# An S4 mixer and MLP kernel: parts of the spectra in the free dimension, taps of two channels per matmul, one transposing transfer per block and chunk

## The chip, the cores and the metric

The kernel runs on one core of a Trainium2 chip. TensorE (PE) multiplies matrices into PSUM; VectorE (DVE), ScalarE (ACT) and GpSimd (POOL) compute on SBUF; SyncE (SP) issues nearly all transfers. The metric is the device time of one execution in microseconds. The median of three runs of the kernel before is 296.92 us (296.33 to 298.66).

## The reference

x has 2048 positions of 512 channels. Two residual blocks follow each other: a long convolution along the positions, whose taps K come from a state-space model with 128 complex states per channel, and an MLP of width 1376. Cut to what matters:

```python
logdA = dt * (A_re + 1j * A_im); dB = dt * Bc
P = jnp.exp(logdA[:, :, None] * l[None, None, :])     # l = 0..2047, rounded to bf16
K = jnp.einsum("dn,dnl,dn->dl", Cc, P, dB).real       # taps of each channel
y = irfft(rfft(pad(u)) * rfft(pad(K)))[:L] + u * Dskip
h = x + y        # u = layernorm(x)
h2 = h + (gelu(layernorm(layernorm(h)) @ w1 + b1) @ w2 + b2)
```

## The kernel before

**Planner.** Every operation is recorded by `add` with its engine, a cost and what it reads and writes. `Sched.run` then orders all of them by a model of the engines, with priorities from the table RANK and PSUM slots from a pool of four (1024 fp32 each), and the order it finds is emitted per engine. It also models PE's clock and a wait at every 256th PE instruction. Because of the helpers, all evictions from PSUM (`evac`) show as L536 on ScalarE or L538 on VectorE, whichever the planner chose, and all transfers as L548.

**Arena.** SBUF is one array `ar`; buffers are byte ranges in it, and many share bytes at different times. E and I hold, for each of NCH = 4 chunks of 128 channels, the real and imaginary parts of exponentials: 20 rows "A" (EA, IA) and 33 rows "B" (EB, IB).

**Taps.** The exponent of position l is split into one of 20 A rows and one of 33 B rows, so the taps of one channel are a 20 x 33 product over the 128 states. `aexps` makes the magnitudes of A in PSUM tiles that accumulate, each fourth row from the one before (LD, two tiles), with an Exp on ScalarE; `bexps` makes those of B. `chain` accumulates phases in PSUM, takes Sin on ScalarE and multiplies on VectorE (L1013, L1014). `kgen` (L1035, L1036) multiplies per channel: 20 weight columns, 33 moving columns, real and imaginary part accumulating, four channels in four column tiles of PE. It evicts into Kg (three buffers). `kspec` (L1080) applies the weights W (a cosine and sine transform along one digit of the position) to Kg over 20 rows in four row tiles, evicts into AK (two buffers) and writes to AK_d in DRAM. `kload` reads it back with the other digit on the partitions and does the second transform stage (L1096).

**Spectra of u.** `austage` does the first stage for the normalised input and writes AU_d in DRAM; `xspec0` (block 0, all channels, L917) and `xspec` (block 1, one chunk at a time, L935) read it back and do the second stage. The stage's weights T have 64 columns of a real and 64 of an imaginary part for each f, so that both parts of a spectrum lie on the partitions. A third copy of 64 columns lets `TT_` form a matmul with the parts swapped, and so each spectrum is kept twice, as X and as Xs. Block 1 uses two buffer pairs XB and two KF1 for the four chunks.

**Inverse.** `inverse` multiplies the tap spectrum with X and Xs on VectorE (L1114), transforms back with TP1 and TP2 over 128 rows (L1123) and evicts into Z. For six of the eight calls, Z is written to Z_d in DRAM and read back into ZT with (q, f) on the partitions. For chunks 2 and 3 of block 0 (TURN) the matmul has its operands exchanged, the result is evicted in four pieces, transposed by PE (L1138) and evicted again.

**Tail and MLP.** `tail` adds x and the last inverse stage in PSUM (L1208, L1213), takes statistics on VectorE (L1218), normalises (L1232, L1234) and transposes (L1239). `mlp` follows: L1257 with Gelu (L1259), then L1274 and the residual (L1276). Each 1024 positions (block) have two tails and two MLP passes. Block 0's taps act on block 0; block 1 needs the taps and spectra of both.

Of the kernel before, what the change touches and what calls it, by code (L numbers as in the profile page):

```python
# [9 lines left out]
ACT = mybir.ActivationFunctionType  # L10
# [13 lines left out]
NKG = 3  # L24
# [124 lines left out]
class VS(V):  # L149
# [15 lines left out]
    "0S": 4, "0A": 87, "0.01A": 322, "0.02S": 140, "0.03A": 55, "0.04S": 263, "0.05S": 334, "0.1S": 264, "0.1A": 228, "0P": 137, "0.05P": 299,  # L165
    "0.1D": 85, "0.7D": 202, "0.75P": 153, "0.6P": 340, "0.72P": 246, "0.3D": 22, "0.1P": 309, "0.2P": 335, "0.05A": 239, "0.06A": 339, "0.07A": 247,
    "0.08A": 330, "0.09A": 269, "0.5D": 304, "0.5P": 353, "0.2A": 341, "0.2D": 96, "1.01A": 359, "1.015A": 184, "1.02A": 238, "1.025A": 240,
    "1.03A": 59, "1.035A": 251, "1.04A": 208, "1.045A": 24, "1.05A": 116, "1.055A": 75, "1.06A": 150, "1.065A": 49, "1.07A": 106, "1.075A": 349,
    "1.08A": 162, "1.085A": 40, "1.09A": 35, "1.095A": 104, "1.1A": 237, "1.105A": 213, "1.11A": 79, "1.115A": 102, "1.12A": 338, "1.125A": 326,
    "1.13A": 220, "1.135A": 115, "1.14A": 180, "1.145A": 42, "1.15A": 205, "1.155A": 90, "1.16A": 278, "1.165A": 361, "0.4A": 84, "0.4P": 229,  # L170
    "0.401A": 163, "0.4D": 12, "0.41D": 21, "0.42D": 274, "0.6A": 291, "0.6D": 248, "0.5S": 13, "0.55D": 44, "0.55S": 261, "1.5D": 317, "1.3P": 307,
    "1.55D": 354, "1.4P": 206, "1.5P": 38, "1.2D": 3, "1.201D": 60, "1.202D": 195, "1.203D": 172, "8D": 270, "8S": 165, "0.95P": 64, "0.95A": 110,
    "1.05P": 320, "1.15P": 305, "1.25P": 54, "1.25A": 127, "1.35P": 157, "1.35A": 99, "1.45P": 232, "1.45A": 289, "1.55P": 315, "1.55A": 188,
    "1.65P": 257, "1.65A": 161, "1.75P": 187, "1.75A": 10, "1.85P": 105, "1.85A": 37, "8A": 7, "1.3A": 70, "1.3D": 345, "1.7P": 32, "1.71P": 266,
    "1.9A": 114, "2.05P": 221, "1.8P": 133, "1.81P": 192, "2.11P": 145, "2P": 199, "2A": 211, "2D": 178, "2.1P": 203, "2.1A": 262, "2.1D": 46,
    "2.2P": 357, "2.2A": 210, "2.2D": 28, "2.3P": 48, "2.3A": 19, "2.3D": 148, "2.5P": 119, "2.5A": 61, "2.5D": 181, "2.6P": 355, "2.6A": 168,
    "2.6D": 36, "2.7P": 66, "2.7A": 300, "2.7D": 83, "2.8P": 113, "2.8A": 128, "2.8D": 234, "2.9P": 301, "2.9A": 212, "2.9D": 135, "2.94A": 89,
    "3.2D": 225, "4.1D": 280, "2.98A": 132, "2.99D": 86, "2.96A": 325, "2.97A": 362, "2.95A": 303, "4.5P": 151, "1.72P": 292, "3.4D": 302,
    "3.401D": 124, "3.402D": 313, "3.403D": 209, "3.5P": 53, "3.5A": 231, "3.5S": 173, "3.501P": 43, "3.501A": 295, "3.501S": 6, "4P": 306, "4A": 268,
    "4D": 243, "4.1P": 58, "4.1A": 65, "4.2P": 324, "4.2A": 319, "4.2D": 57, "4.3P": 242, "4.3A": 103, "4.3D": 331, "4.5A": 108, "4.5D": 236,  # L180
    "4.6P": 332, "4.6A": 218, "4.6D": 15, "4.7P": 226, "4.7A": 297, "4.7D": 352, "4.8P": 71, "4.8A": 73, "4.8D": 179, "4.9P": 155, "4.9A": 189,
    "4.9D": 277, "4.1S": 327, "4.101P": 283, "4.101A": 154, "4.101S": 97, "4.2S": 69, "4.201P": 351, "4.201A": 216, "4.202P": 344, "4.202A": 107,
    "4.203P": 50, "4.203A": 201, "5.1P": 166, "5.1A": 316, "5.11P": 29, "5.11A": 1, "5.11D": 147, "5.2P": 146, "5.2A": 190, "5.2S": 88, "6.2P": 260,
    "6.2A": 214, "6.2S": 20, "5.25S": 275, "5.25P": 33, "5.25A": 77, "5.3D": 170, "5.3P": 204, "5.3A": 284, "5.3S": 139, "9.1P": 25, "9.1A": 39,
    "9.11P": 346, "9.11A": 323, "9.11D": 167, "9.2P": 253, "9.2A": 136, "9.2S": 272, "10.2P": 224, "10.2A": 196, "10.2S": 23, "9.25S": 318,
    "9.25P": 68, "9.25A": 347, "9.3D": 142, "9.3P": 254, "9.3A": 62, "9.3S": 185, "13.1P": 56, "13.1A": 30, "13.11P": 81, "13.11A": 348, "13.11D": 174,
    "13.2P": 31, "13.2A": 94, "13.2S": 249, "14.2P": 227, "14.2A": 342, "14.2S": 333, "13.25S": 294, "13.25P": 45, "13.25A": 296, "13.3D": 76,
    "13.3P": 329, "13.3A": 169, "17.1P": 98, "17.1A": 120, "17.11P": 130, "17.11A": 121, "17.11D": 186, "17.2P": 143, "17.2A": 175, "17.2S": 52,
    "18.2P": 197, "18.2A": 215, "18.2S": 271, "17.25S": 217, "17.25P": 158, "17.25A": 112, "17.3D": 152, "17.3P": 285, "17.3A": 308, "25S": 11,
    "25.02S": 336, "25.04S": 259, "25.06S": 360, "25.1S": 82, "25.12S": 51, "25.14S": 356, "25.16S": 41, "40S": 92, "40.1S": 267, "40.2S": 67,  # L190
    "40.3S": 255, "40.5S": 95, "40.51S": 17, "40.52S": 256, "40.53S": 200, "40.54S": 350, "40.55S": 118, "40.56S": 138, "40.57S": 123, "40.58S": 282,
    "40.59S": 250, "42A": 343, "42P": 80, "30P": 288, "30D": 74, "30A": 279, "31P": 252, "31D": 273, "31A": 233, "70P": 290, "70A": 293, "70D": 122,
    "70S": 314, "50S": 111, "50P": 276, "50A": 194, "51S": 337, "51P": 244, "51A": 328, "52D": 141, "52P": 281, "52A": 14, "52S": 193, "53S": 5,
    "53P": 93, "53A": 101, "54S": 126, "54P": 182, "54A": 27, "55D": 9, "55P": 191, "55A": 0, "55S": 156, "56S": 286, "56P": 223, "56A": 47,
    "57S": 310, "57P": 134, "57A": 16, "58D": 241, "58P": 125, "58A": 129, "58S": 72, "59S": 159, "59P": 171, "59A": 149, "60S": 235, "60P": 258,
    "60A": 312, "61D": 8, "61P": 222, "61A": 198, "61S": 311, "65S": 245, "65.02S": 34, "65.04S": 219, "65.06S": 164, "65.1S": 18, "65.12S": 117,
    "65.14S": 144, "65.16S": 26, "71P": 298, "71A": 91, "71D": 183, "71S": 265, "66P": 2, "66D": 78, "66A": 176, "67P": 358, "67D": 160, "67A": 177,
    "73P": 131, "73A": 207, "73D": 230, "73S": 109, "74P": 321, "74A": 287, "74D": 100, "74S": 63,
# [33 lines left out]
class Sched:  # L232
# [45 lines left out]
    def run(self, nslots):  # L278
# [47 lines left out]
        while av:  # L326
# [84 lines left out]
def kernel(ctx, tc, A_u, A_A_re, A_A_im, A_B_re, A_B_im, A_C_re, A_C_im, A_log_dt, A_Dskip,  # L411
# [509 lines left out]
    def TT_(f, r):  # L921
        return T.ap()[:, f, r:r + 2].rearrange("p a b -> p (a b)")

# [481 lines left out]
```

## Time and profile before

| | |
|---|---|
| median of 3 runs | 296.92 us |
| the profiled execution | 297.31 us, of it span 295.5 us |
| PE, busy | 232.2 us (79%), 3337 matmuls |
| VectorE, busy | 185.5 us (63%), 392 instructions |
| ScalarE, busy | 198.0 us (67%), 257 instructions |
| GpSimd, busy | 46.0 us (16%) |
| DMA | 34.15 MB in 57191 packets, 43873 of them under 512 B |
| evictions of 1024 fp32 values | ScalarE 61 at 1.03 us, VectorE 31 at 1.22 us |

Busy times of PE overlap its weight loads, and matmuls are pipelined, so a busy PE need not be at its peak. The chain of waits goes back from the last instruction to what released each step. "issue" in it is time in which an engine waited for nothing that the profile shows. In the table of stretches each row gives busy time and count for each engine, then the granted PE clock, the mean busy share of the 16 DMA engines and the GB/s.

### The profile page before, as it was taken

How to read it: one execution, taken by the hardware profiler on the slowest of the kernel's cores; microseconds unless marked ns; L12 is line 12 of the kernel's file. 1: busy time of each engine (PE TensorE's matmuls, PEld its weight loads, DVE VectorE, ACT ScalarE, POOL GpSimd, SP SyncE). 2: the span in 40 equal slices, each digit the busy share in tenths (PEclk: the TensorE clock that was granted, in tenths of full speed). 3: DMA queues.
4: the chain of work that ended last, by engine and by line, in shares of the span. 5: the costliest groups of instructions: out<-in, count | busy, mean ns of one | idle time of the engine just before them, and what ended most of it. 6: DMA issues, size and time to landing. Idle time of an engine off the chain costs nothing.

```text
span 295.5 us, 8030 instructions
## 1 busy us (share of the span) xinstructions
PE 232.2 (79%) x3337; PEld 140.1 (47%) x3360; DVE 185.5 (63%) x392; ACT 198.0 (67%) x257; POOL 46.0 (16%) x213
## 2 busy tenths in 40 slices
PE   6204948788997797499977629799999999898983
PEld 2101313344576546487855226578674334443431
DVE  3999999999986798035736784656850375311021
ACT  5988999999956994157984848685528338832700
POOL 9992102996000000000000000000000000000000
PEclk9999998999999999979999958999999999999999
DMA  7700113799101679997896300656564011002011
GB/s 145 265 0 2 35 41 91 195 231 341 35 4 57 192 167 241 239 235 257 249 219 155 71 1 0 176 141 201 144 159 110 0 46 29 1 18 57 0 35 36
DMA packets 57191, 34.15 MB, mean 116 GB/s; under 512 B 43873, under 2 KB 52034, under 8 KB 57154
## 3 DMA queue, kind: packets, MB, share of 16 engines
q1 hardware_dynamic: 55954, 33.24, 42.3%
q8 instruction: 26, 0.43, 0.6%
q10 hardware_dynamic: 1200, 0.39, 0.5%
q14 instruction: 11, 0.09, 0.1%
HBM read 19.47 MB, written 13.63 MB: 112 GB/s over the span
## 4 chain that ended last, share of the span: by engine, by line
PE 47%; DVE 22%; issue 10%; ACT 9%; DMA 5%; SPq 3%; POOL 2%; DVEq 0%; ACTq 0%; POOLq 0%
PE ps L1274 12%; PE ps L1257 9%; ACT ar L536 6%; PE ps L1123 5%; DVE ar L593 4%; PE ps L1036 3%; SPq L548 3%; PE ps L1035 3%; DVE ar L878 3%; DVE ar L598 3%; DVE ar L538 3%; PE ps L997 2%; PE ps L1080 2%; DMA ar<-AU_d 2%; DVE ar L1218 2%
## 5 line engine op out<-in xcount | busy, mean ns | idle before, releaser
L536 ACT CAST ar<-ps 128x1024 bf16<-128x1024 f32 (+3 forms) x91 | 75.2, 889 | 49.5 <-DVE ar L1218 9.8
L538 DVE CAST ar<-ps 128x1024 bf16<-128x1024 f32 (+2 forms) x33 | 38.8, 1194 | 19.0 <-PE ps L1096 12.8
L1257 PE MATMUL ps<-ar 128*128 128x512 bf16 (+1 forms) x170 | 40.6, 384 | 2.8 <-ACT ar L536 1.4
L1274 PE MATMUL ps<-ar 128*128 128x512 bf16 (+1 forms) x168 | 40.1, 379 | 3.1 <-DVE ar L1276 2.7
L1114 DVE TENSOR_TENSOR ar<-ar 128x1024 bf16<-128x1024 bf16 x48 | 30.1, 688 | 17.1 <-PE ps L1123 14.6
L1259 ACT ACTIVATE ar<-ps,ar 128x512 bf16<-128x512 f32 (+1 forms) x44 | 29.7, 689 | 14.5 <-PE ps L1257 14.1
L1003 ACT ACTIVATE ar<-ps 128x1024 bf16<-128x1024 int16 x36 | 35.5, 1042 | 3.5 <-PE ps L997 3.0
L584 POOL TENSOR_SCALAR ar<-ar 128x128 bf16<-128x128 bf16 (+5 forms) x40 | 30.5, 783 | 15.6 <-DMA ar<-ar 10.4
L1276 DVE TENSOR_TENSOR ar<-ps,ar 128x512 bf16<-128x512 f32 x16 | 11.0, 690 | 32.7 <-PE ps L1274 25.6
L1257 PEld LDWEIGHTS <-ar 128*128 128x128 bf16 (+1 forms) x176 | 17.6, 101 | 22.1 <-issue 4.3
L1274 PEld LDWEIGHTS <-ar 128*128 128x128 bf16 (+1 forms) x176 | 16.7, 97 | 22.8 <-issue 4.9
L1036 PE MATMUL ps<-ar 128*20 128x33 bf16 x512 | 20.0, 248 | 6.6 <-issue 6.6
L1218 DVE BATCH_NORM_STATS2 ar<-ps 128x6 f32<-128x512 f32 x16 | 11.1, 697 | 21.7 <-PE ps L1213 16.7
L1123 PE MATMUL ps<-ar 128*128 128x128 bf16 x384 | 24.1, 219 | 0.6 <-DVE ar L1114 0.3
L997 PE MATMUL ps<-ar 128*32 128x256 f16 x560 | 21.4, 275 | 3.8 <-ACT ar L1003 1.6
L1123 PEld LDWEIGHTS <-ar 128*128 128x128 bf16 x384 | 22.3, 98 | 3.3 <-DVE ar L1114 1.0
L1036 PEld LDWEIGHTS <-ar 128*20 128x20 bf16 x512 | 17.8, 125 | 8.2 <-issue 8.2
L997 PEld LDWEIGHTS <-ar 128*32 128x32 f16 x560 | 13.9, 97 | 12.6 <-issue 12.1
L1035 PE MATMUL ps<-ar 128*20 128x33 bf16 x512 | 19.7, 249 | 0.2
L1014 DVE TENSOR_TENSOR ar<-ar 128x1024 bf16<-128x1024 bf16 x26 | 17.8, 702 | 1.6 <-ACT ar L1003 1.5
L1013 DVE TENSOR_TENSOR ar<-ar 128x1024 bf16<-128x1024 bf16 x26 | 18.1, 709 | 0.9 <-ACT ar L1003 0.8
L1035 PEld LDWEIGHTS <-ar 128*20 128x20 bf16 x512 | 17.5, 124 | 0.5 <-issue 0.2
(92 smaller groups left out, 307.8 us busy)
## 6 DMA issues: line engine op xcount, KB each, us to landing
AU_d<-ar SPq DMA_DIRECT2D x16, 256.0 KB, 4.6
ar<-AU_d SPq DMA_DIRECT2D x8, 512.0 KB, 5.9
AK_d<-ar SPq DMA_DIRECT2D x16, 256.0 KB, 4.2
ar<-AK_d SPq DMA_DIRECT2D x8, 512.0 KB, 5.6
Z_d<-ar SPq DMA_DIRECT2D x12, 256.0 KB, 3.2
ar<-Z_d SPq DMA_DIRECT2D x6, 512.0 KB, 4.6
ar<-in_A_u_dram SPq DMA_DIRECT2D x4, 512.0 KB, 7.1
ar<-in_A_u_dram SPq DMA_DIRECT2D x16, 128.0 KB, 5.4
```

The lines of the kernel that those rows point to most:

```text
L536: act.copy(out_fn(), in_fn())
L538: dve.tensor_copy(out_fn(), in_fn())
L584: en.tensor_scalar(a, b, f(s1), f(s2), op0, op1)
L997: pe.matmul(pst(p)[32 * g:32 * g + 32, 256 * j:256 * j + 256], lhsT=W2[DELTAS.index(d)].ap(), rhs=S2[g].ap()[:, ch0:ch0 + 256], start=Fals ...
L1003: add("ACT", c_act(1024), lambda e, p=p, sc=sc, cs=cs: act.activation(sc[cs].ap().rearrange("p a b -> p (a b)"), pst(p, i16).rearrange("p ...
L1035: pe.matmul(o, lhsT=Ar.ap()[:, :, d], rhs=Br.ap()[:, :, d], start=True, stop=False, tile_position=(0, 32 * g))
L1036: pe.matmul(o, lhsT=Ai.ap()[:, :, d], rhs=Bi.ap()[:, :, d], start=False, stop=True, tile_position=(0, 32 * g))
L1114: add("DVE", c_dve(1024, 2), lambda e, kf=kf, x=x, pr_=pr_, f0=f0: dve.tensor_tensor(pr_.ap(), kf[f0:f0 + 8].ap(), x[f0:f0 + 8].ap(), ALU. ...
L1123: pe.matmul(pst(p)[:, 128 * k:128 * k + 128], lhsT=a, rhs=b_, start=(n == 0), stop=(n == len(jobs) - 1))
L1257: pe.matmul(pst(p)[:fs, 512 * z:512 * z + 512], lhsT=w1s[dc].ap()[:, fc * P:fc * P + fs], rhs=ybuf.ap()[:, dc, :], start=(dc == 0), stop=( ...
L1259: add("ACT", c_act(512, 1), lambda e, p=p, z=z, fc=fc, fs=fs: act.activation(hT.ap()[:fs, fc, :], pst(p)[:fs, 512 * z:512 * z + 512], ACT. ...
L1274: pe.matmul(pst(p)[:, 512 * z:512 * z + 512], lhsT=hT.ap()[:fs, fc, 128 * t:128 * t + 128], rhs=w2s[fc].ap()[:fs], start=(fc == 0), stop=( ...
```

## The change

The second stage now makes real and imaginary parts side by side in the free dimension (two matmuls of 64 weight columns, one in each half of PE's columns, for two values of f). The swapped spectrum is no copy any more but a reversed index in the product. The inverse contracts over 64 rows in two row tiles with three half-size tables TP, always with the channels on the output partitions, and one transfer per block and chunk transposes Z from SBUF to SBUF; Z_d, TURN's path and Xs are gone. `kgen` handles two channels per matmul: 52 weight columns (12 rows that are padding or an earlier buffer's end, then 20 rows of each channel) by 66 moving ones; the cross products are left unused, and W is zero on the first 12 rows. `aexps` uses three PSUM tiles (each sixth row from the one before), and EA and IA keep the two halves of a chunk's channels apart. Kg and AK have four buffers, XB and KF1 four each. RANK has new values, and two constants of the planner's model change.

```diff
-NKG = 3
+NKG = 4
 RANK = {
...
-                        blk.append(t + 2.8 + 0.6 * min(8.0, max(0.0, dma_busy - t)))
+                        blk.append(t + 3.3 + 0.4 * min(5.0, max(0.0, dma_busy - t)))
...
-    T = take(bf16, 16, 3, 64)
-    TP1 = take(bf16, 16, P)
-    TP2 = take(bf16, 16, P)
+    T = take(bf16, 16, 2, 64)
+    TP = [take(bf16, 8, P) for _ in range(3)]
...
-    XR = [(VS(X0, c), VS(X0s, c)) for c in range(NCH)]
-    Kg = [take(bf16, NB, 32) for _ in range(NKG)]
-    AK = [take(bf16, 16, CW) for _ in range(2)]
+    XR = [VS(X0, c) for c in range(NCH)]
+    Kg = [take(bf16, NB, 2, 32) for _ in range(2)] + [at(lo, bf16, NB, 2, 32) for lo in (X0s.lo, BA0 + 12288)]
+    AK = [take(bf16, 16, CW) for _ in range(2)] + [at(BA0 + 4096 * n, bf16, 16, CW) for n in (1, 2)]
...
-    EA = [at(E0 + c * ESZ, bf16, NA, CW) for c in range(NCH)]
+    EA = [at(E0 + c * ESZ, bf16, 2, NA, 64) for c in range(NCH)]
...
-        for f in range(16):
+        for f in range(8):
...
-                    pe.matmul(pst(p)[:, 512 * r:512 * r + 512], lhsT=TT_(f, r), rhs=X0.ap()[:, f, :], start=True, stop=True)
...
-            evac(lambda f=f: multi(X0.lo + 1024 * f, 16384, bf16, 2, 512), lambda p=p: pst(p).rearrange("p (c d) -> p c d", c=2), 1024, [p], [X0[f], X0s[f]])
+                    for h in range(2):
+                        fmat(pst(p)[64 * h:64 * h + 64, 512 * r:512 * r + 512], 2 * f + h, r, X0.ap()[:, 2 * f + h, :])
...
+            evac(lambda f=f: X0[2 * f:2 * f + 2].ap().rearrange("p a b -> p (a b)"), lambda p=p: pst(p), 1024, [p], [X0[2 * f:2 * f + 2]])
+    def fmat(o, f, r, rhs):
+        pe.matmul(o, lhsT=T.ap()[:, f, r, :], rhs=rhs, start=True, stop=True, tile_position=(0, 64 * (f & 1)))
+    def fstage(v):
+        for f0 in range(0, 16, 8):
...
+                for k in range(0, 8, 2):
+                    for r in range(2):
+                        for h in range(2):
+                            fmat(pst(p)[64 * h:64 * h + 64, 128 * (k + r):128 * (k + r) + 128], f0 + k + h, r, v.ap()[:, f0 + k + h, :])
...
+        fstage(X)
...
-    KIS = [[(0, 11), (11, 11)], [(22, 10)]]
+    KIS = [[(0, 7), (7, 7)], [(14, 7), (21, 7)], [(28, 4)]]
...
+                    for i in range(n):
+                        for z, (a, b) in enumerate(pair):
+                            for t in range(2):
+                                o = pst(p)[64 * t:64 * t + 32 + NA, 512 * nb:512 * nb + 2 * NB * n].rearrange("p (k i) -> p k i", i=n)[:, :, i]
+                                pe.matmul(o, lhsT=a[:, :, 32 * t + i0 + i], rhs=b[:, :, :, 32 * t + i0 + i], start=(z == 0), stop=(z == 1), tile_position=(0, 64 * t))
...
+        fstage(kf)
...
-            for kf, (X, Xs) in pairs:
-                for x, TPx in ((X, TP1), (Xs, TP2)):
+            for kf, X in pairs:
+                for sw in range(2):
...
+                        a, b_, o = (q.ap().rearrange("p (a r) d -> p a r d", r=2) for q in (kf[f0:f0 + 8], X[f0:f0 + 8], pr_))
+                        dve.tensor_tensor(o, a, b_[:, :, ::-1, :] if sw else b_, ALU.mult)
...
+                for k in range(4):
+                    for n, (q, w0, w1) in enumerate(jobs):
+                        for r, w in enumerate((w0, w1)):
+                            for h in range(2):
+                                rows = slice(64 * h, 64 * h + 64)
+                                b_, a = TP[w].ap()[rows, f0 // 2 + k, :], q.ap()[rows, 2 * k + r, :]
+                                pe.matmul(pst(p)[:, 512 * h + 128 * k:512 * h + 128 * k + 128], lhsT=a, rhs=b_, start=(n == 0 and r == 0), stop=(n == len(jobs) - 1 and r == 1), tile_position=(64 * h, 0))
...
-            evac(lambda z=z: z.ap().rearrange("p a b -> p (a b)"), lambda p=p: pst(p), 1024, [p], [z])
-            dma("SP", lambda z=z, f0=f0: Z_d[b][c][:, f0:f0 + 8, :], lambda z=z: z.ap(), 262144, [z], [("Z", b, c, fh)])
...
-        dma("SP", lambda: zt.ap(), lambda: zv, 524288, [("Z", b, c, 0), ("Z", b, c, 1)], [zt], k=1.2)
+            evac(lambda f0=f0: zw.ap()[:, :, f0:f0 + 8].rearrange("p q (k h) -> p q k h", h=2), lambda p=p: pst(p).rearrange("p (h k q) -> p q k h", h=2, k=4), 1024, [p], [zw])
+        add("SP", 0.55, lambda e: nc.sync.dma_start(zt.ap(), zw.ap().rearrange("p (s q) f -> p s (q f)", s=16), transpose=True), r=[zw], w=[zt], byts=524288)
...
-    XB = [(at(BA0 + 26624 + 8192 * n, bf16, 16, CW), at(BA0 + 26624 + 8192 * n + 4096, bf16, 16, CW)) for n in range(2)]
-    KF1 = [at(BA0 + 43008 + 4096 * n, bf16, 16, CW) for n in range(2)]
+    XB = [at(BA0 + 26624 + 4096 * n, bf16, 16, CW) for n in range(4)]
+    KF1 = [at(lo + 4096 * n, bf16, 16, CW) for lo in (BA0 + 43008, X0s.lo) for n in range(2)]
...
-    Jk = at(Kg[0].lo, f32, 16, 64)
+    Jk = at(Kg[0].lo, f32, 8, 64)
...
-    TS(T, T, 1.0, None, ALU.mult, n=1024, mode=4, oap=lambda: T.ap()[:, :, 2, :], iap=lambda: T.ap()[:, :, 0, :], pr=2.99)
-    AC(TP1, TPc[0], ACT.Sin, scale=pmS, oap=lambda: TP1.ap().rearrange("p a b -> p (a b)"), iap=lambda: low16(TPc[0]), tbl=True, pr=2.96)
-    AC(TP2, TPc[1], ACT.Sin, scale=SINSC, oap=lambda: TP2.ap().rearrange("p a b -> p (a b)"), iap=lambda: low16(TPc[1]), tbl=True, pr=2.97)
+    for n, (q, sc) in enumerate(((0, SINSC), (0, -SINSC), (1, SINSC))):
+        AC(TP[n], TPc[q], ACT.Sin, scale=sc, oap=lambda n=n: TP[n].ap().rearrange("p a b -> p (a b)"), iap=lambda q=q: low16(TPc[q]), tbl=True, pr=2.96 + 0.003 * n)
...
-        inverse(1, c, [(KF0[c], XB[c % 2]), (KF1[c % 2], (XR[c][0], XR[c][1]))], ZT1[c], 2 * c, 52 + 3 * c)
+        inverse(1, c, [(KF0[c], XB[c]), (KF1[c], XR[c])], ZT1[c], 52 + 3 * c)
```

## The prediction

> **What bounds the kernel now.** The profiled execution took 297.31 us (span 295.5, so 1.8 lie around it); the median of the runs is 296.92. I sum against 297.3 and carry the difference over. First I read busy time by stretch of 20 us (columns: length; busy us and instructions of PE, its weight loads, VectorE, ScalarE, GpSimd; granted clock; DMA share; GB/s).
>
> ```profile
> 60.00:80.00 20.00, 17.41 (x314) 9.23 (x314) 19.68 (x30) 19.55 (x22) 11.14 (x13) 1.00 0.70 214
> 80.00:100.00 20.00, 17.10 (x726) 14.65 (x718) 14.82 (x26) 13.83 (x17) 0.52 (x1) 1.00 0.22 62
> 100.00:120.00 20.00, 15.41 (x420) 10.26 (x417) 16.46 (x18) 14.50 (x16) 0.00 (x0) 1.00 0.86 205
> 120.00:140.00 20.00, 16.52 (x507) 14.13 (x496) 6.36 (x9) 9.49 (x12) 0.00 (x0) 0.91 0.92 240
> 140.00:160.00 20.00, 16.30 (x380) 14.10 (x377) 12.74 (x16) 17.31 (x22) 0.00 (x0) 1.00 0.84 221
> 160.00:180.00 20.00, 10.74 (x83) 5.80 (x74) 14.06 (x53) 12.07 (x18) 0.00 (x0) 0.75 0.19 44
> ...
> 200.00:220.00 20.00, 19.79 (x220) 14.32 (x222) 14.95 (x22) 8.93 (x11) 0.00 (x0) 1.00 0.57 158
> ```
>
> Four regimes: up to 80 us VectorE and ScalarE are full; from 80 to 160 no engine is, but DMA is at 0.84 to 0.92; from 160 to 180 (the first tails) PE is half idle at a low clock; from 180 on PE is full. Next, the chain of waits (start, length, what) and the waits of PE's weight loads, where a row is who waited for whom, us, times, longest.
>
> ```profile
> 108.43 5.27 DMA ar<-AK_d
> 113.75 1.07 PE ps L1096 x16
> ...
> 118.69 1.09 issue
> ...
> 122.11 2.77 issue
> ...
> 143.49 3.41 ACT ar L536 x4
> ...
> 157.86 1.11 PE ps L1138 x16
> ...
> 199.37 1.84 PE ps L1123 x32
> ...
> 231.19 0.56 PE ps L1213 x4
> ```
>
> ```profile
> PEld L1036 <- issue: 8.2, 8, 2.9
> ```
>
> The DMA view (queue: packets, MB, share; then issues with count, size, us to landing):
>
> ```profile
> q8 instruction: 26, 0.43, 0.6%
> ...
> AK_d<-ar SPq DMA_DIRECT2D x16, 256.0 KB, 4.2
> ar<-AK_d SPq DMA_DIRECT2D x8, 512.0 KB, 5.6
> Z_d<-ar SPq DMA_DIRECT2D x12, 256.0 KB, 3.2
> ar<-Z_d SPq DMA_DIRECT2D x6, 512.0 KB, 4.6
> ```
>
> The middle stretch is a sequence of latencies: `kgen` on PE with gaps in which PE has nothing to issue, trips through AK_d, evictions on ScalarE. The gaps fit instruction fetch: 26 packets carry 0.43 MB, 16.5 KB each, and PE's 3337 matmuls with 3360 loads in 26 portions are 258 instructions each. `kgen` has 1024 matmuls and 1024 loads, 8 such portions, and 8 gaps of 8.2 us together. The chain shows four of its matmuls every 0.07 us, so a portion lasts 128 x 17.5 ns = 2.24 us, less than its successor takes to come while DMA is loaded.
>
> **Part by part.** *Taps.* `kgen` goes from 1024 matmuls (20 weight columns, 33 moving, four column tiles) to 512 (52 and 66, two tiles). If issue alone sets the pace, 17.5 ns each, it falls from 17.9 to 9.0 us; if weight columns do, 17.5 x 52/20 = 45.5 ns and 23.3 us. I take the moving columns, 35 ns and 17.9 us as before: twice the columns at half the tiles, between the ends. A portion of 256 instructions then lasts 4.5 us, and there are 4: half of the gaps go, **-4.1**, all on the chain (bounds 0 and -8.2). Its evictions grow from 726 + 330 to 924 + 924 + 264 elements per chunk: at 773 ns per 726 some 1.1 us more per chunk, hidden by ScalarE, which is busy for 9.5 of 20 us there; without that cover it is +4.4.
>
> *Spectra.* `xspec0` drops from 16 evictions of 1024 to 8, `xspec` of block 1 from 16 to 8; the swapped copy Xs is now read by a reversed access pattern. The chain products already read reversed blocks (L1013, 709 ns) and cost what the plain ones do (688 ns), so the 48 products stay. A ScalarE eviction is 1.03 us, one on VectorE 1.22. From 98 to 112 us both engines evict back to back; eight fewer over two engines would be -4.5, but the AK_d trip ends last there, so I take half, **-2.2** (0 to -4.5). From 138 to 150 us ScalarE does 14 evictions in 12.07 us; four fewer, partly given back by VectorE, **-2.0** (0 to -4.1). On PE, two 64-wide column tiles overlap: four matmuls of 512 columns in 0.56 us (L1213) against 4 x 0.223 (32 of L1257 in 7.14), 0.63 of serial. So block 1's 128 `xspec` matmuls cost 35 ns for 56, 4.5 us for 7.2; `kload`'s 128 become 256, 9.0 for 7.2: about nothing in sum (3.6 us better if fully paired, 7.1 worse if serial).
>
> *Inverse.* 384 matmuls over 128 rows (32 in 1.8 us, 56 ns) become 768 over 64 rows in two row tiles. L1080 has four row tiles: 16 matmuls of 256 columns and 48 of 128 in 1.22 us (at 158.97 in the chain), against 4.5 us at 56 ns per 128 columns one after another, 3.7 of 4. For two I take 1.8: 31 ns, 23.8 us for 21.5. Two thirds lie in block 1, where PE is full: **+1.5** (0 to +14 if not paired at all: 256 more x 56 ns).
>
> *Transfer.* Six trips of Z through DRAM (12 writes, 6 reads) and, for chunks 2 and 3 of block 0, 32 PE transposes with 12 evictions become eight transfers from SBUF to SBUF that transpose. No row shows such a transfer. A packet took 42.3% x 16 x 295.5 us / 55954 = 36 ns. If its packets are 256 B, like those of the Z read, 2048 of them over 16 engines are 4.6 us, as the Z read takes to land; at 128 B 9.1; at 2 B 585; from below, the 32 KB ar<-ar copies land in 1.9. I take the Z read, of equal size and nearest, 4.6. In block 0 the last chunk decides: from its last matmul (157.1) over eviction, transposes and eviction to the tail's first matmul (160.1) takes 3.0 us; an eviction of 1.03, issue and 4.6 take 5.7: **+2.7** (0 to +7.2). Chunks 0 and 1 lose their writes, chunk 2 has slack. On SP one issue (0.33 to 0.38 us each) replaces three; it waits for the chunk's second eviction, and behind it in SP's queue stand AK_d transfers and loads of x, for which `kload` and the tails wait. In block 1 MLP work covers all but nothing of the last one: the second tail runs amid MLP matmuls until 247. [...]
>
> *Buffers.* XB and KF1 go from two to four, Kg to four, AK to four. Before, the third and fourth block-1 spectra were fetched at 185.6 and 196.9, after XB came free; now they can be fetched in the 160 to 180 hole, where DMA is at 0.19. That takes up to 64 x 72 ns + 32 x 66 ns = 6.7 us out of the stretch where PE is full; VectorE and ScalarE have statistics to do in the hole, so **-4** (0 to -6.7).
>
> *Setup.* Half-size Jk and codes, no copy of T, three table sines of 1024 for two of 2048, against two more weights for `aexps` and a few short VectorE operations: **-0.5**. The new RANK reorders everything; I price it at nothing.
>
> Sum: -4.1 - 2.2 - 2.0 + 1.5 + 2.7 - 4 - 0.5 = -8.6; 297.3 - 8.6 = 288.7, or **288** against the median. With all good ends (-8.2 - 4.5 - 4.1 - 6.7 - 0.5, the rest 0) it would be 273; half of that further way, 280, is the good end that I allow, and 294 the other end of this case.
>
> **The rivals.** *The transposing transfer is slow* (the slower side). From 95 to 160 us the DMA shares, read in steps of 5 us, come to 55.5 of 65 us: 10 us are free, and two Z trips (2304 packets each, 5.1 us) are removed. Four transfers of L each fit until 4L = 20 plus the gain of about 11 made elsewhere: it decides from L = 8 us. With 128 B packets, L = 9.1, the four cost 36.6 - 20 = 16, in place of the 2.7: 302; with 64 B packets the time is far above 320. For: no row, and a transpose must break rows up. Against: SBUF at both ends. Chance 0.22. [...]
>
> *Narrow weights load slowly*: the pace of column tiles is set by weight columns. From the 17.5 ns of 20 columns, 52 cost 45.5 and 64 cost 56: `kgen` +5.4, `kload` +7.1, gaps as I have them; 288 + 12.5 minus the 3 us that fall into the hole is 297. For: 1024 loads in the same time as the matmuls. Against: the 0.56 us of L1213. Chance 0.12. [...]
>
> *DMA holds the middle stretch*: shortening `kgen` and evictions only moves waits to AK_d, so the 8.3 us of the first three terms shrink to 2: 294. For: shares of 0.95 to 1.05 from 110 to 130 in those steps. Chance 0.08.
>
> **How the numbers follow.** My case, 280 to 294, has 0.58. Within 1% of 296.92 is 294 to 299.9, about what a measurement can tell from no change. Faster: 0.58 and half of the DMA rival, 0.62. Same: the other half and most of the weights rival, 0.13. Slower: the transfer and the rest, 0.25. The range 278 to 302 leaves out half of the transfer rival and a little below.
>
> **What would show it.** `kgen` in half the matmuls with some 4 us of issue gaps; first tail statistics near 156 us, not 161.6; a transposing transfer landing in 4 to 6 us; AU_d reads before 185. A landing above 8 us, `kgen` over 23 us, or a first tail at 160 or later makes it wrong.

## The result and the profile after

The kernel after takes 315.5 us in the median of four runs (314.1 to 316.9), the kernel before 297.8 on the same chip (296.3 to 299.2): a ratio of 1.060, 95% interval 1.051 to 1.068. It is slower by some 18 us where 288 was forecast. The profiled execution took 316.26 us, its span is 314.5; before it was 297.31 and 295.5.

Busy time by stretch of 20 us, kernel after (columns as in the table of before):

```profile
80.00:100.00 20.00, 19.48 (x274) 13.36 (x275) 15.44 (x25) 15.15 (x16) 0.00 (x0) 1.00 0.68 212
100.00:120.00 20.00, 19.67 (x404) 16.10 (x402) 13.09 (x18) 13.81 (x16) 0.52 (x1) 1.00 0.41 114
120.00:140.00 20.00, 19.75 (x418) 18.36 (x414) 5.07 (x8) 8.53 (x10) 0.00 (x0) 1.00 0.75 182
140.00:160.00 20.00, 13.36 (x450) 11.13 (x448) 10.85 (x13) 10.39 (x11) 0.00 (x0) 0.96 0.96 210
160.00:180.00 20.00, 11.31 (x257) 9.82 (x257) 8.48 (x11) 12.11 (x13) 0.00 (x0) 0.76 1.10 246
180.00:200.00 20.00, 12.47 (x135) 7.39 (x136) 11.06 (x42) 10.25 (x14) 0.00 (x0) 0.67 0.45 120
```

From 80 to 140 us PE is now full, where it had 15.4 to 17.1 us of 20 before; from 140 to 180 DMA is full (0.96 and 1.10) and PE works for 13.4 and 11.3 us of 20. The hole of the first tails, 160 to 180 us before, has moved to 180 to 200. The groups of `kgen` (busy, mean ns | idle before), before and then after, the waits of its weight loads after, and pieces of PE's timeline (start, length, what, how many), before and then after, say why PE is full:

```profile
L1036 PE MATMUL ps<-ar 128*20 128x33 bf16 x512 | 20.0, 248 | 6.6 <-issue 6.6
L1035 PE MATMUL ps<-ar 128*20 128x33 bf16 x512 | 19.7, 249 | 0.2
```

```profile
L1065 PE MATMUL ps<-ar 128*52 128x66 bf16 x512 | 34.1, 304 | 0.1
L1065 PEld LDWEIGHTS <-ar 128*52 128x52 bf16 x512 | 32.2, 178 | 2.2 <-issue 1.9
```

```profile
PEld L1065 <- issue: 1.9, 8, 0.4
```

```profile
80.00 0.25 PE L1035 MATMUL ps<-ar 128*20 128x33 bf16 x4
80.07 0.26 PE L1036 MATMUL ps<-ar 128*20 128x33 bf16 x4
```

```profile
86.28 1.95 PE L1065 MATMUL ps<-ar 128*52 128x66 bf16 x28
```

The issue gaps fell from 8.2 to 1.9 us, but half as many matmuls now keep PE busy for 34 us. In the timeline 28 of them take 1.95 us: (1.95 - 0.304) / 27 = 61 ns each, 512 x 61 ns = 31 us. Before, four started every 0.07 us, 17.5 ns each, and 1024 x 17.5 ns were 18. What this does to SP's queue shows in its own timeline (start, length with waits for room, what, how many), kernel after:

```profile
102.72 0.47 SPq L552 DMA_DIRECT2D ar<-in_A_u_dram  x1
111.71 1.29 SPq L552 DMA_DIRECT2D ar<-in_B_w_dram  x3
114.57 9.17 SPq L552 DMA_DIRECT2D ar<-in_A_u_dram  x12
123.84 3.61 SPq L552 DMA_DIRECT2D AK_d<-ar  x4
...
151.56 3.26 SPq L1156 DMA_TRANSPOSE ar<-ar  x1
...
161.58 5.21 SPq L1156 DMA_TRANSPOSE ar<-ar  x1
...
173.26 6.14 SPq L1156 DMA_TRANSPOSE ar<-ar  x2
```

Between 103.2 and 111.7 SP issues nothing. The view of waits for 100 to 130 us, restricted to SP, names what it waited for (us in total, times, longest):

```profile
SPq L552 <- PE ps L1065: 9.5, 2, 8.6
```

A load of MLP weights into a taps buffer waits for `kgen` to have read it; behind it in the queue stand twelve loads of x, and behind those the first write to AK_d, at 123.8 us. Before, it was at 102.1:

```profile
102.05 1.01 SPq L548 DMA_DIRECT2D AK_d<-ar  x2
```

So DMA lies half idle while PE works, and is the bound afterwards. The same window of both kernels, before and then after, 100 to 137 and 137 to 188 us (second last column: DMA share):

```profile
100.00:137.00 37.00, 29.03 (x862) 21.60 (x856) 20.49 (x23) 21.36 (x25) 0.00 (x0) 0.95 0.90 217
137.00:188.00 51.00, 37.89 (x561) 27.48 (x562) 33.74 (x79) 38.48 (x51) 0.00 (x0) 0.90 0.46 124
```

```profile
100.00:137.00 37.00, 36.67 (x740) 32.29 (x738) 15.49 (x21) 20.03 (x22) 0.52 (x1) 1.00 0.54 141
137.00:188.00 51.00, 32.72 (x830) 25.58 (x828) 23.40 (x30) 27.71 (x30) 0.00 (x0) 0.81 1.02 229
```

In the first window DMA does (0.90 - 0.54) x 37 = 13 us less than before; the second is full of it, with shares between 0.86 and 1.18 in steps of 5 us. At the end of that window comes the last transposing transfer of block 0. The chain of waits shows its issue (start, length, what) and then goes on in a read of AK_d that stood behind it; the DMA view gives the landing of these transfers:

```profile
177.58 1.82 SPq L1156
179.57 4.83 DMA ar<-AK_d
```

```profile
ar<-ar SPq DMA_TRANSPOSE x8, 4.3
```

The 4.3 is a median, and the smallest and the largest are 4.3 as well, so it may be the landing of few of the eight. The last eviction of chunk 3 and the first tail's matmul that reads it, in the timeline (in brackets: the engine's idle time before, and what ended it):

```profile
174.34 1.01 ACT L540 CAST ar<-ps 128x1024 bf16<-128x1024 f32 x1 [0.20 <-PE ps L1153]
182.06 0.64 PE L1226 MATMUL ps<-ar 128*64 128x512 bf16 x2 [5.49 <-DMA ar<-ar]
```

From the end of that eviction, 175.4, to the matmul are 6.7 us: 2.2 behind the transposing issue of chunk 2 on SP, 4.5 from its own issue. The first tail's statistics, before and then after:

```profile
161.62 0.70 DVE L1218 BATCH_NORM_STATS2 ar<-ps 128x6 f32<-128x512 f32 x1 [1.92 <-PE ps L1213]
183.84 0.70 DVE L1231 BATCH_NORM_STATS2 ar<-ps 128x6 f32<-128x512 f32 x1 [5.44 <-PE ps L1226]
```

From there to the end of the span it takes 130.7 us, before 133.9: after the tail the change gains 3 us. The whole loss lies ahead of it.

### The profile page after: what moved, and what is told of

Read it like the earlier page. It is cut to its first block, busy times and chain, and to the rows that moved or that the text cites. A ratio compares the mean times of both kernels' runs of the same rounds, so it can differ in the third digit from the quotient of the medians.

```text
span 314.5 us, 7976 instructions
## 1 busy us (share of the span) xinstructions
PE 249.5 (79%) x3332; PEld 151.6 (48%) x3332; DVE 181.0 (58%) x390; ACT 188.7 (60%) x243; POOL 40.9 (13%) x218
## 5 line engine op out<-in xcount | busy, mean ns | idle before, releaser
L1142 DVE TENSOR_TENSOR ar<-ar 128x1024 bf16<-128x1024 bf16 x48 | 30.0, 685 | 29.6 <-ACT ar L540 13.6
L542 DVE CAST ar<-ps 128x1024 bf16<-128x1024 f32 (+3 forms) x29 | 32.2, 1118 | 20.3 <-PE ps L931 5.7
L1065 PE MATMUL ps<-ar 128*52 128x66 bf16 x512 | 34.1, 304 | 0.1
L1065 PEld LDWEIGHTS <-ar 128*52 128x52 bf16 x512 | 32.2, 178 | 2.2 <-issue 1.9
L931 PE MATMUL ps<-ar 128*64 128x128 bf16 (+1 forms) x416 | 21.9, 263 | 9.1 <-DMA ar<-AU_d 6.9
L1270 PEld LDWEIGHTS <-ar 128*128 128x128 bf16 (+1 forms) x176 | 17.5, 102 | 21.6 <-issue 3.2
L1153 PE MATMUL ps<-ar 64*128 64x128 bf16 x768 | 24.7, 216 | 1.8 <-ACT ar L540 1.2
L1153 PEld LDWEIGHTS <-ar 64*128 64x128 bf16 x768 | 21.8, 94 | 6.4 <-issue 4.1
L931 PEld LDWEIGHTS <-ar 128*64 128x64 bf16 x416 | 16.5, 131 | 13.0 <-DMA ar<-AU_d 7.1
L749 ACT ACTIVATE ar<-ar 128x512 bf16<-128x512 f32 x32 | 17.3, 616 | 3.0 <-DVE ar L597 3.0
L597 DVE TENSOR_TENSOR ar<-ar 128x4 f32<-128x4 f32 (+7 forms) x59 | 15.5, 271 | 4.0 <-POOL ar L652 2.5
```

Source lines behind the costliest of these rows:

```text
L542: dve.tensor_copy(out_fn(), in_fn())
L931: pe.matmul(o, lhsT=T.ap()[:, f, r, :], rhs=rhs, start=True, stop=True, tile_position=(0, 64 * (f & 1)))
L1065: pe.matmul(o, lhsT=a[:, :, 32 * t + i0 + i], rhs=b[:, :, :, 32 * t + i0 + i], start=(z == 0), stop=(z == 1), tile_position=(0, 64 * t))
L1142: dve.tensor_tensor(o, a, b_[:, :, ::-1, :] if sw else b_, ALU.mult)
L1153: pe.matmul(pst(p)[:, 512 * h + 128 * k:512 * h + 128 * k + 128], lhsT=a, rhs=b_, start=(n == 0 and r == 0), stop=(n == len(jobs) - 1 and ...
L1270: pe.matmul(pst(p)[:fs, 512 * z:512 * z + 512], lhsT=w1s[dc].ap()[:, fc * P:fc * P + fs], rhs=ybuf.ap()[:, dc, :], start=(dc == 0), stop=( ...
```

## Experiments

Each ratio is to the kernel before on the same chip. "First tail" is the start of the first tail statistics in the profiled execution. "New order" means that RANK was searched anew, with the planner's prices set as told; the same work then runs in another order. Times are medians; the ratios are worked out from the single executions and need not be the quotient of two medians. Where the first tail is blank, the profiled execution can't be compared with the others.

| run | time, us | ratio | 95% interval | first tail |
|---|---|---|---|---|
| after | 315.5 | 1.060 | 1.051 to 1.068 | 183.8 |
| e1 adjacent tap operands, order of after | 302.0 | 1.016 | 1.010 to 1.022 | 171.4 |
| e2 adjacent weights alone (one run) | 310.9 | | | 180.7 |
| e3 plain copy for the transpose, order of after | 309.0 | 1.035 | 1.026 to 1.045 | 175.3 |
| e7 after, new order | 302.6 | 1.019 | 1.011 to 1.028 | 169.7 |
| e17 e7 with adjacent tap operands | 298.8 | 1.000 | 0.997 to 1.004 | 168.9 |
| e11 before, new order | 299.0 | 1.001 | 0.997 to 1.005 | 162.1 |
| e18 before, another new order | 301.2 | 1.015 | 1.009 to 1.020 | 162.9 |
| e5 transfers alone, ranks of before | 305.5 | 1.033 | 1.024 to 1.043 | 171.0 |
| e16 transfers alone, new order | 293.4 | 0.984 | 0.980 to 0.989 | 160.9 |
| e6 spectra and transfers, taps as before, new order | 300.3 | 1.014 | 1.007 to 1.021 | 171.3 |
| e8 e6, chunk 3 turned by PE | 298.8 | 1.001 | 0.997 to 1.005 | 167.7 |
| e9 e7, chunk 3 turned by PE | 298.5 | 0.998 | 0.994 to 1.002 | 167.5 |
| e12 e6, chunks 2 and 3 turned by PE | 294.0 | 0.984 | 0.980 to 0.989 | 164.8 |
| e10 spectra alone, Z through DRAM for chunks 0 and 1, by PE for 2 and 3, new order | 293.0 | 0.983 | 0.978 to 0.987 | 163.0 |
| e13 e10 with two channels per tap matmul | 293.2 | 0.982 | 0.977 to 0.987 | 165.3 |
| e15 Z of chunks 0 to 2 through DRAM, chunk 3 by PE | 295.7 | 0.990 | 0.985 to 0.995 | |
| e14 all chunks by PE | 296.8 | 0.991 | 0.987 to 0.995 | |

**The pace of the taps.** Theory A: the tap matmuls take twice the time forecast, and that is most of the loss. Rival B: the transposing transfers are. e1 gives both operands of the tap matmuls adjacent elements, e2 the weights alone; the order is that of after. The elements are then not those that the taps need: both runs keep the work and leave out the right taps.

```diff
-pe.matmul(o, lhsT=a[:, :, 32 * t + i0 + i], rhs=b[:, :, :, 32 * t + i0 + i], start=(z == 0), stop=(z == 1), tile_position=(0, 64 * t))
+pe.matmul(o, lhsT=a[:, i0 + i, 0:52], rhs=b[:, 66 * (32 * t + i0 + i):66 * (32 * t + i0 + i) + 66], start=(z == 0), stop=(z == 1), tile_position=(0, 64 * t))   # e1
+pe.matmul(o, lhsT=a[:, i0 + i, 0:52], rhs=b[:, :, :, 32 * t + i0 + i], start=(z == 0), stop=(z == 1), tile_position=(0, 64 * t))   # e2
```

> The changed kernel, its order of instructions unchanged, but both operands of kgen's matmuls read 52 and 66 adjacent elements instead of one element from each row (the taps are then wrong numbers; nothing else is left out). Theory A, the pace of the taps: kgen's 61 ns per matmul come from moving columns that lie 128 B apart, about 1.67 ns each in two column tiles; adjacent ones go at about 0.42 ns, so 20 to 30 ns per matmul, PE gets 15 to 20 us back between 86 and 137 us, and most of the 18 us come back: 298 to 303 us. Theory B, the transposing transfers: SP is held 3 to 6 us by each while AK_d transfers queue behind it, and DMA is full from 137 to 188 us; faster taps only make PE wait longer, 308 us or more.

> As e1, but only kgen's weights are adjacent; the 66 moving elements stay 128 B apart (wrong taps again). If moving columns set the pace (theory A) it stays at 58 to 62 ns per matmul and the time within 2 us of the changed kernel. If the weight loads set it, it falls below 45 ns and the time by 8 us or more.

The group of `kgen` and one piece of PE's timeline, in e1 and then in e2:

```profile
L1065 PE MATMUL ps<-ar 128*52 128x66 bf16 x512 | 16.7, 249 | 0.1
```

```profile
109.20 6.80 PE L1065 MATMUL ps<-ar 128*52 128x66 bf16 x224
```

```profile
L1065 PE MATMUL ps<-ar 128*52 128x66 bf16 x512 | 30.7, 291 | 0.1
```

```profile
115.48 12.89 PE L1065 MATMUL ps<-ar 128*52 128x66 bf16 x224
```

With adjacent operands a tap matmul takes 30 ns (6.80 us for 224), and the time falls from 1.060 to 1.016, by 4.3% or 13 us, with the order untouched, as theory A had it. In e2 it still takes 57 ns (12.89 us for 224): of the 31 ns between strided and adjacent operands the weights are worth 4, and the moving columns, with the weights adjacent in both runs, 27. In these runs the pace is in the main that of the moving columns. The weights count for more than theory A allowed: it had 58 to 62 ns and a time within 2 us of after, and e2's single execution is 4.6 us below after. Per moving column of a pair of tiles, 2 x 61 / 66 = 1.85 ns became 2 x 30 / 66 = 0.9, where theory A had 1.67 and 0.42. Mean durations lead to the same two numbers: 66 strided columns 304 ns (after) and 33 strided 249 (before) are (304 - 249) / 33 = 1.67 ns for a strided column, and 512 adjacent ones 379 (L1274 before) and 128 adjacent 219 (L1123 before) are (379 - 219) / 384 = 0.42 for an adjacent one. In e1 66 adjacent columns have a mean of 249 ns.

**The transpose in the transfer.** e3 moves the same 512 KB without transposing.

```diff
-nc.sync.dma_start(zt.ap(), zw.ap().rearrange("p (s q) f -> p s (q f)", s=16), transpose=True)
+nc.sync.dma_start(zt.ap(), zw.ap().rearrange("p (s q) f -> p s (q f)", s=16))
```

> The changed kernel with the eight transfers from SBUF to SBUF not transposing: the same 512 KB copied partition by partition (Z then has the wrong layout, nothing is left out). Theory A: the transposing transfer is about as cheap as it was priced, so this gains at most 4 us: 311 to 316. Theory B: SP is free again and DMA gets room, so 298 to 305.

Landing and SP's issues in e3:

```profile
ar<-ar SPq DMA_DIRECT2D x8, 512.0 KB, 2.9
```

```profile
147.77 0.68 SPq L1156 DMA_DIRECT2D ar<-ar  x1
156.59 0.51 SPq L1156 DMA_DIRECT2D ar<-ar  x1
```

The plain copy lands in 2.9 us (again one value for smallest and largest) and holds SP for 0.5 and 0.7 in the two issues shown; the transposing one in after lands in 4.3 and holds it for 3.3, 5.2, 4.2 and 1.8 us in block 0. That is worth 2.4% (7 us) in the order of after, between the two expectations: more than theory A's 4 us, and not the whole loss. The profiled execution of e3 is its fastest, 305.4 us, so its first tail is early.

**The order.** e7 is after, every instruction the same, with the planner's price of a tap matmul at 61 ns in place of 30 and of a transposing issue at 2.5 us of SP in place of 0.55, and RANK searched with them. e6 also puts the taps back to one channel per matmul. e17 is e7 with e1's operands; e11 and e18 are the kernel before in two other orders of the same planned length.

```diff
-                add("PE", 0.12 * n, fn, r=res, w=[p], new=[p] if nb == 0 else [])
+                add("PE", 0.24 * n, fn, r=res, w=[p], new=[p] if nb == 0 else [])
-        add("SP", 0.55, lambda e: nc.sync.dma_start(zt.ap(), zw.ap().rearrange("p (s q) f -> p s (q f)", s=16), transpose=True), r=[zw], w=[zt], byts=524288)
+        add("SP", 2.5, lambda e: nc.sync.dma_start(zt.ap(), zw.ap().rearrange("p (s q) f -> p s (q f)", s=16), transpose=True), r=[zw], w=[zt], byts=800000)
```

> The kernel after, every instruction the same, only the planner's prices (tap matmul 61 ns in place of 30, transposing issue 2.5 us) and with them the ranks searched anew: the order alone changes. Theory A (the tap matmuls' 30 us stand on the path in any order): 308 to 314. Rival B (the order was laid out for taps of half their real price, and that order is most of the loss): 303 or less.

> The kernel after with the taps again by one channel per matmul in four column tiles of 33 columns (as before), spectra and transfer as after; the ranks searched anew with prices from the traces (17.5 ns a tap matmul, a transposing issue 2.5 us of SP). Theory A (the doubled price of the tap matmuls is the bulk of the loss): taps 18 us busy, ending near 122, time 297 to 304. Rival B (the loss lies mostly in what is kept: spectra and transfers): over 308. Should the spectra's part bring what was forecast for it and the transfer cost no more than 3 us, it comes out under 297.

> The reordered kernel after (302.6, ratio 1.019), same order, the operands of the tap matmuls adjacent, so that they take 30 ns in place of 61; the taps are then those of other rows. If the doubled tap time is hidden in this order: within 2 us of that run, ratio 1.012 to 1.022. If it still stands on the path: ratio 1.00 or less.

> Control: the kernel before, every instruction the same, its ranks searched further by the same search with its own prices (planned end 284.1 in place of 287.0). If a new search is worth nothing by itself: 294 to 299, and what the other runs gain is their edits. If it is 293 or less, that much of their gain is the order alone.

> Control for the orders: the kernel before once more, every instruction the same, in another order that the planner prices like the first control's (284.07 and 284.06 us). If runs of separately ordered kernels may be compared to within half a per cent: ratio 0.995 to 1.006, as that one (1.001). If two orders of one planned length differ on the chip by more, the pairs of separately ordered kernels tell nothing below that difference, and the gain of the transfer alone in its new order (0.984) may be its order.

e7 fell to 1.019: the order alone is worth 4.0%, 12 us, where theory A had 308 or more. The two windows in e7:

```profile
100.00:137.00 37.00, 36.05 (x736) 32.16 (x733) 16.40 (x21) 22.32 (x26) 1.06 (x3) 1.00 0.74 193
137.00:188.00 51.00, 37.59 (x855) 27.58 (x850) 32.73 (x77) 33.10 (x40) 0.00 (x0) 0.81 0.82 188
```

PE is as full as in after, and yet DMA has moved from the second window into the first (0.54 to 0.74, 1.02 to 0.82): the taps begin at 78.4 us in place of 86.3 and the first AK_d write is issued at 114.9 in place of 123.8. The doubled taps and the order overlap: e1's remedy alone gets back 13 us, e7's alone 12, and both together, in e17, 5.9% (18 us), 1.9% (5.6 us) more than e7. Even in the new order the doubled taps stand partly on the path. e7 changes the price of the tap matmuls, that of the transposing issue and the size of the transfer in the model at once, and searches anew; that the price of the taps is what made the order of after bad is argued, from SP's wait for `kgen`, and not shown.

e6 came out as theory A had it, but e7, with the doubled taps, is only 0.5% above it, so e6 can't tell the taps from the order. e11 shows that a new search is worth nothing by itself; but e18, with a planned length equal to e11's within 0.02 us, is 1.4% slower than it. Two kernels in orders of their own can therefore not be told apart below about 1.4%, 4 us, and that limit comes from one pair of orders; for e1, e3 and e17, which keep an order, this limit doesn't hold.

**The transfers alone.** e4 and e5 put eight transposing transfers into the kernel before, with its ranks; the reads of Z_d and the PE transposes of TURN go too.

```diff
-            evac(lambda z=z: z.ap().rearrange("p a b -> p (a b)"), lambda p=p: pst(p), 1024, [p], [z])
-            dma("SP", lambda z=z, f0=f0: Z_d[b][c][:, f0:f0 + 8, :], lambda z=z: z.ap(), 262144, [z], [("Z", b, c, fh)])
...
+            evac(lambda f0=f0: zw.ap()[:, :, f0:f0 + 8], lambda p=p: pst(p).rearrange("p (f q) -> p q f", f=8), 1024, [p], [zw])
+        add("SP", 0.55, lambda e: nc.sync.dma_start(zt.ap(), zw.ap().rearrange("p (s q) f -> p s (q f)", s=16), transpose=True), r=[zw], w=[zt], byts=524288)
```

> The kernel before, with the transfer alone changed: all eight inverses put the channels on the output partitions, evict once per half into a buffer in the chain's scratch, and transpose by one transfer from SBUF to SBUF; taps, spectra and priorities are those of before. Theory A: within 2% of before, 293 to 302, with the last chunk of block 0 some 3 us later and Z's DRAM traffic gone. Theory B: the middle stretch grows as in the changed kernel, 305 or more.

> The kernel before with only the transfer exchanged: all eight (block, chunk) pairs write the inverse transposed into a 4 KB buffer and move it by one transposing transfer in SBUF; taps, spectra and order as before. The first such run shared its buffers with the half-swapped spectra and so waited falsely; here the second buffer lies where block 1's normalized rows come later. Theory A (the transposing transfer costs some 4 us net, mostly by holding the SP queue 2 to 6 us an issue): 300 to 303. Rival B (the 301.3 of that run came from the shared buffers): within 1.5 us of before, 296 to 299.

> The kernel before with the eight transposing transfers alone, as in the earlier run, but its ranks searched anew with an issue at 2.5 us of SP (planned 287.8, where the reordered kernel before has 284.1). If the transfers themselves cost (a landing and an SP hold ahead of the tail in place of 32 PE transposes): 302 to 305. If most of that run's loss was its order: 297 to 301.

e4 took 301.3 us (1.015, 1.007 to 1.022); its buffers shared bytes with Xs, so part of block 0's spectra was overwritten, and its waits are not those of the edit. e5 took 305.5, above both expectations; e16, the same instructions in a new order, 293.4, below both. The timelines around the last transfer of block 0 tell the two apart, e5 first:

```profile
155.33 9.22 SPq L548 DMA_DIRECT2D AK_d<-ar  x4
...
161.51 1.01 ACT L536 CAST ar<-ps 128x1024 bf16<-128x1024 f32 x1 [0.23 <-PE ps L1125]
161.64 0.11 PEld L1198 LDWEIGHTS <-ar 128*64 128x64 bf16 x1 [0.29 <-issue]
164.59 2.52 SPq L1128 DMA_TRANSPOSE ar<-ar  x1
169.18 0.64 PE L1198 MATMUL ps<-ar 128*64 128x512 bf16 x2 [7.46 <-DMA ar<-ar]
```

```profile
153.64 1.01 ACT L536 CAST ar<-ps 128x1024 bf16<-128x1024 f32 x1 [0.25 <-PE ps L1125]
154.67 2.39 SPq L1128 DMA_TRANSPOSE ar<-ar  x1
...
157.16 1.22 SPq L548 DMA_DIRECT2D AK_d<-ar  x2
...
159.13 0.59 PE L1198 MATMUL ps<-ar 128*64 128x512 bf16 x2 [0.36 <-DMA ar<-ar]
```

In e5 the last inverse comes 8 us later, and its transfer then waits for four AK_d writes that hold SP until 164.6: 6.7 us from the end of the eviction to the tail's matmul. In e16 those writes stand behind the transfer, and it takes 4.5. So the place of the last transfer in SP's queue is worth 2.2 of the 10.1 us between the two first tails; why the last inverse of e5 comes 8 us later isn't shown. The transfers alone are no loss in the order of e16.

**What carries the last chunks.** These runs keep the spectra of the change and vary the rest, each in a new order: chunks turned by 16 PE transposes and two evictions (the path that TURN had), or Z through DRAM as before. The chunks named are turned in both blocks; the kernel before turned chunks 2 and 3 of block 0 only.

```diff
-TURN = (2, 3)
+TURN = (3,)          # e8, e9, e15; (2, 3) in e10, e12, e13; (0, 1, 2, 3) in e14
+        if turn:
+            for sh in range(2):
...
+                        pe.transpose(pst(p, bf16)[:, 128 * s:128 * s + 128], zw.ap().rearrange("p (s q) f -> p s (q f)", s=16)[:, 8 * sh + s, :], identb.ap())
...
+            return
+        dma("SP", lambda: zt.ap(), lambda: zv, 524288, [("Z", b, c, 0), ("Z", b, c, 1)], [zt], k=1.2)     # e10, e13, e15
```

> The run with one channel per tap matmul (300.3), but chunk 3 of each block turned by 16 PE transposes and two evictions, as the kernel before did for chunks 2 and 3, in place of the transposing transfer; ranks searched anew. Theory A (the transposing transfer costs where it is the last thing ahead of the tail: 6 to 8 us from the last inverse eviction to the tail's first matmul against 2 us over TensorE): 291 to 296. Rival B (the loss lies in the transfers' hold of SP and DMA at all chunks): 298 or more.

> The same one edit on the run with two channels per tap matmul in the new order (302.6); ranks searched anew. Theory A: 294 to 298, some 3 us over the one-channel run, of which the doubled tap time hidden in the rest of the order is the difference. Rival B: 300 or more. If taps of 30 us cost their whole excess of 12 us even in a fitting order, 303 or more.

> One channel per tap matmul and Z through DRAM for chunks 0 and 1, by TensorE for chunks 2 and 3, as in the kernel before: of the change only the spectra with parts in the free dimension (no half-swapped copies, row-tiled inverse) is left; ranks searched anew. If the spectra's part gains as forecast (some 4 to 6 us over before): 290 to 294. Rival (the row-tiled inverse and its strided evictions give it back): 296 to 300. Against the run with the last chunk on TensorE it tells what the transposing transfer of the earlier chunks is worth: within 2 us by theory A.

> One channel per tap matmul, spectra of the change, transposing transfers for chunks 0 and 1 alone, chunks 2 and 3 turned over TensorE; ranks searched anew. It differs from the run of the spectra alone (293.0) in nothing but what carries chunks 0 and 1. Theory C (each transposing transfer holds the SP queue and the DMA engines longer, wherever it stands): 296 to 299. Rival D (only the transfers of the last two chunks, next to the tail, cost): 292 to 294.5.

> The run of the spectra alone (293.0) with the taps by two channels per matmul (61 ns each, 31 us); ranks searched anew. By the pair of runs with the last chunk over TensorE (298.7 with one channel, 298.5 with two) the taps' form costs nothing in a fitting order: 292 to 294.5. If the excess of 12 us of TensorE shows: 296 or more. The planner gives it 4 us more.

> The run of the spectra alone with all four chunks of each block turned over TensorE: no Z transfer at all, 32 more PE transposes and 4 more evictions of 1 us in each block; ranks searched anew. Theory C (SP and DMA are the price in 120 to 170 us): 289 to 293. Rival (evictions on ScalarE and VectorE bound that stretch): 294 to 297.

> The run with the last chunk over TensorE (298.7) with Z of chunks 0 to 2 through DRAM in place of the transposing transfers; ranks searched anew. Theory C (the transposing transfer is the dearer transfer): 292 to 295. Rival D' (it was chunk 2, which needs TensorE's short way, by whatever transfer it goes): 297 or more.

e8 (298.8) met the rival's bound, and e9 (298.5) came out between the two. e10 and e13 came as forecast; e12 (294.0) met rival D. From e6 to e12, chunks 2 and 3 by PE, the ratio falls by 2.9%, above the limit of 1.4%; from e7 to e9, chunk 3 alone, by 2.1%. e12 against e10 (0.984 and 0.983) finds transposing transfers of chunks 0 and 1 no dearer than Z through DRAM, and e10 against e13, e8 against e9 find two channels per tap matmul no dearer than one; both within the limit. e15 (295.7) fell between its theories, 1.1% under e8, and e14 (296.8) met its rival's range, 0.9% over e10; both differences lie within the limit too and settle nothing.

e10, e12, e13 and e16 came out faster than both kernels, by 1.6 to 1.8% against before. That is little more than the 1.4% by which an order alone moved the kernel before, and which of the four is best can't be told.

One thing stays open. e16 has the transfers and e10 the spectra, each at 1.6 to 1.8% under before, and e6, which has both with the taps of before, is 1.4% above it. The last transfer is not the reason. In e6:

```profile
162.37 5.67 SPq L1155 DMA_TRANSPOSE ar<-ar  x2
...
163.82 1.01 ACT L540 CAST ar<-ps 128x1024 bf16<-128x1024 f32 x1 [0.25 <-PE ps L1152]
...
169.43 0.64 PE L1225 MATMUL ps<-ar 128*64 128x512 bf16 x2 [3.93 <-DMA ar<-ar]
```

From the end of the eviction to the tail's matmul it takes 4.6 us, as in e16, but the eviction begins at 163.8 in place of 153.6. So the loss of e6 lies ahead of its last inverse. In the chain of waits from 118 to 172 us, issue gaps have 25.0% and a read of AU_d 13.7% in e6; in e16 issue has 5.2% and SP's queue 22.2%. No run takes these apart.

## Why the prediction was wrong

*Taps, -4.1: the step that failed first.* "35 ns ... twice the columns at half the tiles" doubled the 17.5 ns for twice the columns and left out that only two tiles, not four, then run side by side. By the prediction's own numbers that doubles the time per matmul once more, to 70 ns; 61 were measured. Count the matmuls of tiles side by side as one round: 1024 matmuls in four tiles and 512 in two are both 256 rounds. A round took 4 x 17.5 = 70 ns for 33 columns before and 2 x 61 = 122 for 66 after (2 x 30 = 60 for 66 adjacent ones in e1). So `kgen` takes 31 us and not 17.9, +13; the upper bound of 23.3 was too low as well, since it scaled with weight columns. The gaps themselves fell by 6.3, more than the 4.1 forecast. Net +7 of PE time in a stretch in which PE had 3 to 4.6 us idle of 20, and it became the bound there. The prediction had read this stretch, 80 to 160 us, as one with DMA at 0.84 to 0.92; in its own row for 80 to 100, where the taps begin, DMA is at 0.22 and PE works for 17.1 us of 20.

*RANK, "I price it at nothing": a failure as large.* The planner's line for the tap matmuls says 0.12 us for four, 30 ns each, half of what they took. In the order of after, SP waited 8.6 us for `kgen`, and the AK_d writes stood behind twelve loads of x. Same instructions, other order: -4.0%. A table that reorders everything is a part of the change with a price, and the planner's prices, on which it rests, stood in the kernel's own lines.

*What is left.* Taps and order together are 18 us, and e17, which mends both, is at 1.000, where the forecast was 0.97. Some 9 us of the miss lie elsewhere. e9 against e7 (-2.1%) and e12 against e6 (-2.9%), with the last chunks by PE, get back 6 to 9 of them, in orders of their own; which step ahead of the last inverse loses them stays open.

*Transfer, +2.7.* The landing was right, 4.3 us against 4.6, and so was the term where nothing queues: in e16 an eviction of 1.0 and 4.5 to the tail are 5.5 us (5.7 forecast), against 3.0 over PE. What the step missed is the hold of the issue: SP at 0.33 to 0.38 us was the price of a plain transfer, and the transposing one holds it for 1.7 to 5.2 in after. In the order of after, the transpose against a plain copy is 7 us.

*Spectra, buffers, inverse, setup, -7.2 in sum.* Right in sign, and not shown one by one. e10, which has these and chunks 2 and 3 of block 1 by PE, in a new order, is at 0.983, 5 us, known to 4 us for its order. The hoisting is seen: the last block-1 spectra are read at 158.2 in after (196.9 before), and from the first tail to the end it takes 128.6 us in e10 and 128.3 in e7, against 133.9, where -4 was forecast. But the prediction put these reads into the hole of the first tails, where DMA was at 0.19. In after all reads of block 1's spectra were issued from 133.8 to 158.2, in the stretch in which DMA is full; what they cost there no run takes apart. The row-tiled inverse runs as costed, 64 matmuls in 1.89 us, 30 ns each for 31.

*The rivals.* The transposing transfer was not slow in the sense of the rival (L was 4.3, not 8). Weights were not the pace: with 52 weight columns the runs show 61 ns with strided, 57 with the weights alone adjacent, and 30 with both operands adjacent, where the rival had 45.5. The rival with the least chance, DMA holding the middle stretch, is where the loss ended up: a DMA share of 1.02 over 51 us. It was priced as a gain that shrinks to 2 us; nothing in it foresaw that traffic would be pushed into that stretch by work made longer ahead of it.

*The signs it named.* Issue gaps of some 4 us: 1.9. Landing of 4 to 6: 4.3. AU_d reads before 185: 158.2. First tail near 156, wrong at 160 or later: 183.8. `kgen` over 23 us: 31. Of the three marks that it set for being wrong, `kgen` over 23 us and a first tail at 160 or later came; a landing above 8 us did not.

## What to carry to other kernels

Count tiled matmuls in rounds, and look at the moving columns of a round and their stride: here it was 256 rounds before and after, and a round took 70 ns with 33 strided columns, 122 with 66 strided and 60 with 66 adjacent, so half the tiles side by side with twice the columns each brought nothing. Where a planner lays out the order, read its prices against the trace before anything else: here one was wrong by a factor of two, and the order cost as much as the work itself, in waits on queues far from the priced operation. And where two versions run in orders of their own, measure first how much the order alone moves the time: here 1.4% between two orders of one planned length, 4.0% from after to e7 and 4.9% from e5 to e16.

## What the runs showed of the hardware

In the two column tiles of `kgen`, operands that lie apart in SBUF cost time: a tap matmul of 52 weight and 66 moving columns, 128 B from one to the next, took 61 ns in after, 57 with adjacent weights in e2 and 30 with both adjacent in e1.

A transposing transfer from SBUF to SBUF of 512 KB landed in 4.3 us in after, a plain one in 2.9 in e3; the median of the transposing ones was 4.2 in e5, 5.2 in e6 and 6.0 in e9. The transposing issue held SP for 3.3, 5.2, 4.2 and 1.8 us in block 0 of after, where the DMA share is 0.86 to 1.18, and for 1.7 to 3.4 in block 1; a plain copy for 0.5 to 0.7 in e3, in the four issues that stand alone in its timeline.
